# Programs without a Block, one semaphore for the last stores, one load of W2: gated hedgehog attention and MLP on one core

## The chip, the cores and the metric

The kernel runs on one core of a Trainium2 chip. The metric is the device time of one execution in microseconds (us), shown as the median of eight runs. The profile is one further view of the program: one execution recorded by the hardware profiler, with the start and the length of every instruction on the five engines and of every packet of the 16 DMA engines. TensorE is PE in the profile (its weight loads are PEld), VectorE is DVE, ScalarE is ACT, GpSimd is POOL and SyncE is SP. A "q" behind an engine's name (SPq) marks what its sequencer does by itself: issuing transfers, waiting on semaphores, draining, branching.

## What is computed

With S = 2048 rows, D = 512 columns, H = 32 heads of 16 columns, all in bf16:

```python
q, k, v = split_heads(x @ wqkv)                  # H = 32, Dh = 16
pq, pk = q @ w_phi, k @ w_phi                    # per head
phi = lambda p: concat([softmax(p), softmax(-p)])
kv = einsum("bhsf,bhsd->bhfd", phi(pk), v)       # and z: phi(pk) summed over s
o = (phi(pq) @ kv) / (phi(pq) @ z + 1e-6)
a = merge_heads(o) @ wo
b = relu(x @ w1) @ w2                            # Dff = 1376
g = sigmoid((x * gate_w).sum(-1))
return g * a + (1 - g) * b
```

A_x is the x of both branches.

## The kernel before

**How the order comes about.** Nothing schedules this kernel. The function calls `p.op`, `p.dma` and `p.wait` in the order in which each engine is to work, and `_Plan` (lines 14 to 55) keeps one list for each engine. Each entry names the events it has to wait for; `p.dma` counts 16 on the semaphore it is given, `p.op` counts 1 on its engine's. At the end `p.emit` writes one engine's list out: first the waits that this engine has not yet seen fulfilled, then the instruction. SP's list issues all transfers but two; the load of the gate's weights and the very last store are on ACT's.

**Stages.** (1) From the start to about 5 us: x arrives, TensorE runs warm-up products (line 211) and transposes the first 512 rows of x (line 217). (2) To about 18 us: the first products x @ w1 (line 499) and w_phi folded into the q and k weights (`pre`, line 281). (3) To about 83 us, the loop over 16 row tiles (line 551): `atile` (line 300) makes q and k, ACT takes exponentials, DVE sums and inverts, POOL scales, SP transposes phi(q) by DMA (line 375); `kv`, `vtile` and further `hunit`s of x @ w1 fill TensorE. (4) From about 89 us the output loop (line 584): for each row tile `nd` (numerator and denominator), `finB` (h @ w2, eleven matmuls, line 461), `finA` (o @ wo, line 470), the copy to TFA on ACT (line 475), and `comb` (line 480), in which DVE adds the two gated parts and a store goes out.

**What the change touches.** W2, the second layer of the MLP, is loaded in the middle of stage 3, at m = 3 (lines 559 to 565), by three transfers on SP's queue that share the semaphore "w2"; `finB` waits for the last of them (line 464). `comb` stores to one of three output buffers, `ob = m % 3`, each with a semaphore of its own, "out0" to "out2" (line 490), and waits for the store of tile m - 3 before it writes the buffer anew (line 487). The last tile is cut into 384 and 128 columns: the first part goes out on SP, the second on ACT (lines 598 to 602), on semaphores "out0a" and "out0b". SP ends with a wait for four events (line 603). The five lists are emitted into five bodies of one `nc.Block()` (lines 608 to 628). Entering a body is a branch on each engine; leaving the Block is a branch, a drain and a barrier of all engines, which the profile puts down to line 94, where the function's `with` closes. An opening barrier (line 642) stands before the Block and outside the function.

Of the kernel before, what the change touches and what calls it, by code (L numbers as in the profile page):

```python
# [57 lines left out]
def bass_gated_mix__linear_kernel_hedgehog__dense_activation_relu__prompt_kernel(  # L58
# [17 lines left out]
    P = 128  # L76
    NT = S // P
# [13 lines left out]
    KU = KT - 1  # L91
    NR = DFF - KU * P

    with ExitStack() as es:
        E = es.enter_context
# [8 lines left out]
        W2 = E(nc.sbuf_tensor("W2", [P, KT, D], BF16))  # L104
# [34 lines left out]
        p = _Plan(["sp", "pool", "act", "dve", "pe"])  # L139
# [6 lines left out]
        def orow(m):  # L146
            return oq[:, m, :] if m < 4 else o2[m * P:(m + 1) * P, :]
# [14 lines left out]
        for t in range(1, NDT):  # L162
            loadw1(t)
        p.dma("sp", lambda e: e.dma_start(
            out=WPS[:, :, :], in_=A_w_phi.rearrange("(g hl) r c -> (hl r) g c", g=NDT)), "wps", ev="wps")
        p.dma("sp", lambda e: e.dma_start(
            out=WV[:, :, :], in_=A_wqkv[:, 2 * D:3 * D].rearrange("(j p) n -> p j n", p=P)), "wv", ev="wv")
        for i in range(2):
            p.dma("sp", lambda e, i=i: e.dma_start_transpose(
                out=WQKT[:, 4 * i:4 * i + 4, :], in_=A_wqkv[:, i * D:(i + 1) * D]), f"wqk{i}", ev=f"wqk{i}")  # L170
        for c in range(1, NCH):
            p.dma("sp", lambda e, c=c: e.dma_start_transpose(
                out=XT[:, :, c * 512:(c + 1) * 512], in_=x2[c * 512:(c + 1) * 512, :]), f"x{c}", ev=f"x{c}")
# [9 lines left out]
            after=["wps"], ev="wd")  # L183
        for gt in range(NDT):
# [4 lines left out]
                after=["wd", "m8"], ev=f"wbd{gt}")  # L189

        p.op("dve", lambda e: e.tensor_tensor(IDN[:, :], ROWI[:, :], COLI[:, :], ALU.is_equal),
             after=["iota0"], ev="idn")
        p.op("dve", lambda e: e.tensor_single_scalar(ROW8[:, :], ROW8[:, :], 4, ALU.arith_shift_right),
             after=["iota"], ev="r8")
# [3 lines left out]
             after=["r64"], ev="m32")  # L198
# [180 lines left out]
        def vtile(m, eng="act", bank=2):  # L379
            b = m % VB  # L380
            for dt in range(NDT):
                p.op("pe", lambda e, dt=dt: e.matmul(  # L382
                    PS[:, bank, :], XT[:, dt, m * P:(m + 1) * P], WV[:, dt, :],
                    start=(dt == 0), stop=(dt == NDT - 1)),
                    after=((xready(m // 4) + ["wv"] + free[bank]) if dt == 0 else ()),
                    ev=(f"v{m}" if dt == NDT - 1 else None))
            dst, src = VS[:, b, :, 0:64], PS[:, bank, :].rearrange("p (g c) -> p g c", g=NG)
            after = [f"v{m}"] + ([f"kv{m - VB}"] if m >= VB else [])
            if eng == "dve":
                p.op("dve", lambda e: e.tensor_copy(dst, src), after=after, ev=f"cv{m}")  # L390
            else:
                p.op("act", lambda e: e.activation(dst, src, ACT.Copy), after=after, ev=f"cv{m}")  # L392
            free[bank] = [f"cv{m}"]

        def kv(m):
            b = m % NB
            vb = m % VB
            for g in range(NG):
                after = []
                if g == 0:  # L400
                    after = [f"pk{m}", f"cv{m}", f"one{vb}"]
                    if m == 0:
                        after += free[6] + free[7]
                p.op("pe", lambda e, g=g: e.matmul(  # L404
                    PS[:, 6 + g // 4, (g % 4) * GW:(g % 4) * GW + 65],
                    EB[:, b, 3, g * P:(g + 1) * P], VS[:, vb, g, 0:65],
                    start=(m == 0 and g % 4 == 0), stop=(m == NT - 1), skip_group_check=True),
                    after=after, ev=(f"kv{m}" if g == NG - 1 else None))
# [71 lines left out]
        def comb(m, cs=slice(0, 512), tag="", eng="sp"):  # L480
            ob = m % 3
            bank = fbank[(m, tag)]
            n = cs.stop - cs.start
            p.op("dve", lambda e: e.scalar_tensor_tensor(  # L484
                out=OSB[:, ob, cs], in0=PS[:, bank, 0:n], scalar=OMG[:, m:m + 1],
                in1=TFA[:, m % 2, cs], op0=ALU.mult, op1=ALU.add),
                after=[f"fb{m}{tag}", f"ta{m}"] + ([f"out{m - 3}"] if m >= 3 else []), ev=f"cb{m}{tag}")
            free[bank] = [f"cb{m}{tag}"]
            p.dma(eng, lambda e: e.dma_start(out=orow(m)[:, cs], in_=OSB[:, ob, cs]),
                  f"out{ob}{tag}", after=[f"cb{m}{tag}"], ev=f"out{m}{tag}")  # L490


        UB = (3, 4, 5, 0, 6, 7, 2, 1)
# [51 lines left out]
        def unit(c, k):  # L545
            if k < 0:
                rest(c)
            else:
                hunit(c, k)

        for m in range(NT):
            atile(m)
            if m >= LAG:
                kv(m - LAG)
            if m + 3 < NT:
                vtile(m + 3)
            for u in mid[m]:
                unit(*u)
            if m == 3:
                for i in range(2):  # L560
                    a, b = (0, 6) if i == 0 else (6, KU)
                    p.dma("sp", lambda e, a=a, b=b: e.dma_start(
                        out=W2[:, a:b, :], in_=B_w2[a * P:b * P, :].rearrange("(j p) n -> p j n", p=P)),
                        "w2", ev=f"w2{i}")
                p.dma("sp", lambda e: e.dma_start(out=W2[0:NR, KU, :], in_=B_w2[KU * P:DFF, :]), "w2", ev="w2")
            if m == 5:
                p.dma("sp", lambda e: e.dma_start(
                    out=WO[:, :, :], in_=A_wo.rearrange("(j p) n -> p j n", p=P)), "wo", ev="wo")
# [15 lines left out]
        for m in range(NT):  # L584
            if m > 1 and m + 3 < NT:
                nd(m + 3)
            if m + 1 < NT - 1:
                finB(m + 1, FB[(m + 1) % 3])
            if m == 1:
                nd(m + 3)  # L590
            if m == 0:
                nd(2)
                nd(3)
            finA(m, (6, 2, 0)[max(m - NT + 3, 0)])
            if m < NT - 1:
                comb(m)
        m = NT - 1
# [2 lines left out]
            finB(m, (4, 3)[i], cs, "ab"[i])  # L600
        for i, cs in enumerate(cuts):
            comb(m, cs, "ab"[i], ("sp", "act")[i])
        p.wait("sp", [f"out{m}" for m in range(NT - 3, NT - 1)] + [f"out{NT - 1}a", f"out{NT - 1}b"])

        sems = {}
        for name in p.count:
            sems[name] = nc.alloc_semaphore(f"s_{name}")
        block = E(nc.Block())

        @block.sync  # L610
        def _(eng):
            p.emit("sp", eng, sems)

        @block.gpsimd
        def _(eng):
            p.emit("pool", eng, sems)

        @block.scalar
        def _(eng):
            p.emit("act", eng, sems)  # L620

        @block.vector
        def _(eng):
            p.emit("dve", eng, sems)

        @block.tensor
        def _(eng):
            p.emit("pe", eng, sems)


# [26 lines left out]
```

## Time and profile before

| | us |
|---|---|
| median of 8 runs | 150.17 |
| lowest, highest of them | 149.64, 150.44 |
| the profiled execution: its time | 149.96 |
| its span, first to last instruction | 148.2 |
| busy in the span: PE | 144.0 (97%) |
| DVE | 93.2 (63%) |
| ACT | 72.1 (49%) |
| POOL | 52.1 (35%) |

The page cuts the span into 40 equal slices. A digit is the busy share of a slice in tenths, 9 meaning 90% or more; PEclk is the granted TensorE clock in tenths of full speed:

```profile
PE   7999999999999999999999999999999999999991
DVE  2427946777688878678698968655555555544242
ACT  3307627887778778887878861121111111111150
POOL 2040001788768678688869801200000000000000
PEclk9999999999999999999999999999999999999999
```

TensorE is full from the second slice to the last but one, at full clock. All the other engines have gaps. A slice is 3.7 us, so the last one, with a 1 for PE, is the time in which the output's tail leaves the chip. The page's third part names the DMA queues:

```profile
q1 hardware_dynamic: 44496, 15.92, 47.7%
q8 instruction: 8, 0.13, 0.4%
q10 hardware_dynamic: 152, 0.03, 0.1%
q14 instruction: 5, 0.04, 0.1%
```

The columns are packets, MB, and the packets' time as a share of the 16 DMA engines' span. q1 carries what SP issues, q10 what ACT issues; q8 and q14 bring the engines' own instructions.

### The profile page before, as it was taken

How to read it: one execution, taken by the hardware profiler on the slowest of the kernel's cores; microseconds unless marked ns; L12 is line 12 of the kernel's file. 1: busy time of each engine (PE TensorE's matmuls, PEld its weight loads, DVE VectorE, ACT ScalarE, POOL GpSimd, SP SyncE). 2: the span in 40 equal slices, each digit the busy share in tenths (PEclk: the TensorE clock that was granted, in tenths of full speed). 3: DMA queues.
4: the chain of work that ended last, by engine and by line, in shares of the span. 5: the costliest groups of instructions: out<-in, count | busy, mean ns of one | idle time of the engine just before them, and what ended most of it. 6: DMA issues, size and time to landing. Idle time of an engine off the chain costs nothing.

```text
span 148.2 us, 2544 instructions
## 1 busy us (share of the span) xinstructions
PE 144.0 (97%) x978; PEld 73.4 (50%) x978; DVE 93.2 (63%) x157; ACT 72.1 (49%) x123; POOL 52.1 (35%) x62
## 2 busy tenths in 40 slices
PE   7999999999999999999999999999999999999991
PEld 2544744444545545555554545554444444444451
DVE  2427946777688878678698968655555555544242
ACT  3307627887778778887878861121111111111150
POOL 2040001788768678688869801200000000000000
PEclk9999999999999999999999999999999999999999
DMA  4999993033349994335734331454142232333211
GB/s 159 293 270 213 196 221 63 0 71 71 75 82 329 183 180 74 72 70 108 75 71 95 82 71 40 89 114 116 48 98 71 71 75 71 80 91 79 71 66 47
DMA packets 44661, 16.12 MB, mean 109 GB/s; under 512 B 39304, under 2 KB 44008, under 8 KB 44648
## 3 DMA queue, kind: packets, MB, share of 16 engines
q1 hardware_dynamic: 44496, 15.92, 47.7%
q8 instruction: 8, 0.13, 0.4%
q10 hardware_dynamic: 152, 0.03, 0.1%
q14 instruction: 5, 0.04, 0.1%
HBM read 4.41 MB, written 2.10 MB: 44 GB/s over the span
## 4 chain that ended last, share of the span: by engine, by line
PE 96%; DVE 1%; issue 0%
PE PS L461 25%; PE PS L253 19%; PE PS L307 17%; PE PS L470 9%; PE PS L382 9%; PE PS L499 5%; PE PS L436 3%; PE PS L404 3%; PE PS L211 2%; PE PS L265 2%; PE PS L287 1%; PE PS L217 1%; DVE WQK L484 1%; DVE XT L227 1%; PE PS L205 0%
## 5 line engine op out<-in xcount | busy, mean ns | idle before, releaser
L461 PE MATMUL PS<-W,HT 128*128 128x512 bf16 (+4 forms) x187 | 40.6, 366 | 0.0
L326 ACT ACTIVATE EB<-PS 128x480 bf16<-128x480 f32 (+1 forms) x44 | 30.1, 756 | 15.9 <-PE PS L307 15.9
L350 POOL TENSOR_TENSOR EB<-EB,SC 128x1024 bf16<-128x1024 bf16 x15 | 28.9, 1929 | 25.1 <-DVE SC L348 25.1
L475 ACT ACTIVATE TFA<-PS,GT 128x512 bf16<-128x512 f32 x16 | 11.0, 687 | 42.7 <-PE PS L470 36.6
L253 PE MATMUL PS<-XT,W 128*128 128x512 bf16 x128 | 30.7, 379 | 0.0
L307 PE MATMUL PS<-WQK,XT 128*128 128x480 bf16 x128 | 28.5, 366 | 0.0
L484 DVE SCALAR_TENSOR_TENSOR WQK<-PS,OMG,TFA 128x512 bf16<-128x512 f32 (+2 forms) x17 | 12.2, 719 | 23.6 <-ACT TFA L475 22.4
L346 DVE TENSOR_REDUCE ZB<-EB 128x64 f32<-128x1024 bf16 x15 | 18.3, 1220 | 13.9 <-ACT EB L326 13.9
L461 PEld LDWEIGHTS PS<-W,HT 128*128 128x128 bf16 (+1 forms) x187 | 17.1, 98 | 17.4
L239 ACT ACTIVATE HT<-PS 128x512 bf16<-128x512 f32 x35 | 20.3, 614 | 7.7 <-PE PS L499 5.8
L307 PEld LDWEIGHTS PS<-WQK,XT 128*128 128x128 bf16 x128 | 12.5, 98 | 13.8
L361 DVE TENSOR_REDUCE ZB<-EB 128x64 f32<-128x1024 bf16 x16 | 18.6, 1164 | 0.0
L253 PEld LDWEIGHTS PS<-XT,W 128*128 128x128 bf16 x128 | 12.0, 98 | 13.2
L370 POOL TENSOR_TENSOR EB<-EB,SC 128x512 bf16<-128x512 bf16 x16 | 16.9, 1059 | 1.3
L382 PE MATMUL PS<-WV,XT 128*128 128x512 bf16 x64 | 16.2, 378 | 0.0
L470 PE MATMUL PS<-WO,OT 128*128 128x512 bf16 x64 | 16.1, 378 | 0.0
L446 DVE TENSOR_TENSOR WQK<-PS,RDEN 128x512 bf16<-128x512 f32 x16 | 11.1, 692 | 0.5
L470 PEld LDWEIGHTS PS<-WO,OT 128*128 128x128 bf16 x64 | 6.1, 97 | 7.2
L348 DVE RECIPROCAL SC<-ZB 128x64 f32<-128x64 f32 x16 | 8.8, 553 | 0.5
L382 PEld LDWEIGHTS PS<-WV,XT 128*128 128x128 bf16 x64 | 5.5, 97 | 4.9
L392 ACT ACTIVATE VS<-PS 128x512 bf16<-128x512 f32 x13 | 7.9, 609 | 0.0
L499 PE MATMUL PS<-XT,W 128*128 128x512 bf16 x32 | 7.6, 390 | 0.3 <-DVE XT L227 0.2
(55 smaller groups left out, 88.1 us busy)
## 6 DMA issues: line engine op xcount, KB each, us to landing
out_dram<-WQK SPq DMA_DIRECT2D x15, 128.0 KB, 1.7
W<-in_B_w_dram SPq DMA_DIRECT2D x3, 344.0 KB, 5.3
W<-in_B_w_dram SPq DMA_DIRECT2D x1, 768.0 KB, 4.8
OT<-in_A_x_dram SPq DMA_DIRECT2D x2, 256.0 KB, 2.9
WV<-in_A_wqkv_dram SPq DMA_DIRECT2D x1, 512.0 KB, 6.5
W<-in_B_w_dram SPq DMA_DIRECT2D x1, 512.0 KB, 6.1
WO<-in_A_wo_dram SPq DMA_DIRECT2D x1, 512.0 KB, 4.0
PHQ<-EB SPq DMA_TRANSPOSE x16, 2.8
```

The lines of the kernel that those rows point to most:

```text
L239: p.op("act", lambda e: e.activation(dst, src, ACT.Relu), after=[f"h{c}_{kt}"], ev=ev)
L253: p.op("pe", lambda e, t=t: e.matmul(PS[:, bank, :], W1[:, t, kt * P:(kt + 1) * P], XT[:, t, c * 512:(c + 1) * 512], start=(t == 0), stop= ...
L307: p.op("pe", lambda e, dt=dt, which=which: e.matmul(PS[:, which, 0:DE], XT[:, dt, m * P:(m + 1) * P], WQK[:, which, dt * DE:(dt + 1) * DE] ...
L326: p.op("act", lambda e: e.activation(dst, s_, ACT.Exp, scale=scale), after=[f"qk{m}"] + busy, ev=ev)
L346: p.op("dve", lambda e: e.tensor_reduce(zk, ek, AX.X, ALU.add), after=[emk, f"cst{b}"], ev=f"zk{m}")
L350: p.op("pool" if m < NT - 1 else "dve", lambda e: e.tensor_tensor(EB[:, b, 3, :].rearrange("p (g f) -> p g f", f=DH), EB[:, b, 2, :].rearr ...
L361: p.op("dve", lambda e: e.tensor_reduce(ZB[:, b, 0:64].rearrange("p (h s) -> p h s", s=2), bass.AP(tensor=EB, offset=base, ap=[[EBS, P], [ ...
L370: p.op("pool", lambda e: e.tensor_tensor(EB[:, b, 0, :].rearrange("p (h s f) -> p h s f", h=H, s=2)[:, :, 1, :], EB[:, b, 1, :].rearrange( ...
L382: p.op("pe", lambda e, dt=dt: e.matmul(PS[:, bank, :], XT[:, dt, m * P:(m + 1) * P], WV[:, dt, :], start=(dt == 0), stop=(dt == NDT - 1)), ...
L461: p.op("pe", lambda e, kt=kt, M=M: e.matmul(PS[:, bank, 0:n], HT[0:M, kt, m * P:(m + 1) * P], W2[0:M, kt, cs], start=(kt == 0), stop=(kt = ...
L470: p.op("pe", lambda e, t=t: e.matmul(PS[:, bank, :], OT[:, t, m * P:(m + 1) * P], WO[:, t, :], start=(t == 0), stop=(t == NDT - 1)), after ...
L499: p.op("pe", lambda e, u=u: e.matmul(PS[:, UB[u], :], W1[:, t, u * P:(u + 1) * P], XT[:, t, 0:512], start=(t == 0), stop=(t == NDT - 1)), ...
```

## The change

Three edits. The engines' lists are written straight into the program's main block, in the order SP, ACT, TensorE, DVE, POOL; no Block is opened, so there are no branches into bodies and no branch, drain and barrier at the end. Tiles 13, 14 and both parts of tile 15 store on one semaphore, "fin", and SP's closing wait asks for its full count (four stores of 16, so 64). The two loads of W2's full blocks (6 and 4 of them) become one of ten.

```diff
             p.dma(eng, lambda e: e.dma_start(out=orow(m)[:, cs], in_=OSB[:, ob, cs]),
-                  f"out{ob}{tag}", after=[f"cb{m}{tag}"], ev=f"out{m}{tag}")
+                  f"out{ob}" if m < NT - 3 else "fin", after=[f"cb{m}{tag}"], ev=f"out{m}{tag}")
...
             if m == 3:
-                for i in range(2):
-                    a, b = (0, 6) if i == 0 else (6, KU)
-                    p.dma("sp", lambda e, a=a, b=b: e.dma_start(
-                        out=W2[:, a:b, :], in_=B_w2[a * P:b * P, :].rearrange("(j p) n -> p j n", p=P)),
-                        "w2", ev=f"w2{i}")
+                p.dma("sp", lambda e: e.dma_start(
+                    out=W2[:, 0:KU, :], in_=B_w2[0:KU * P, :].rearrange("(j p) n -> p j n", p=P)), "w2", ev="w20")
                 p.dma("sp", lambda e: e.dma_start(out=W2[0:NR, KU, :], in_=B_w2[KU * P:DFF, :]), "w2", ev="w2")
...
-        p.wait("sp", [f"out{m}" for m in range(NT - 3, NT - 1)] + [f"out{NT - 1}a", f"out{NT - 1}b"])
+        p.wait("sp", [f"out{NT - 1}b"])
...
-        block = E(nc.Block())
-
-        @block.sync
-        def _(eng):
-            p.emit("sp", eng, sems)
...
-        @block.tensor
-        def _(eng):
-            p.emit("pe", eng, sems)
+        for name, eng in (("sp", nc.sync), ("act", nc.scalar), ("pe", nc.tensor), ("dve", nc.vector), ("pool", nc.gpsimd)):
+            p.emit(name, eng, sems)
```

The compiled lists differ from those before in nothing else: SP's has one load of W2 less, one wait in place of three entries that waited at its end, and every list is without its two branches, its closing drain and its closing semaphore entries.

More of the change, by code (lines that the diff above doesn't have):

```diff
@@ L607, in bass_gated_mix__linear_kernel_hedgehog__dense_activation_relu__prompt_kernel @@
             sems[name] = nc.alloc_semaphore(f"s_{name}")
-        block = E(nc.Block())
-        @block.sync
-        def _(eng):
-            p.emit("sp", eng, sems)
-        @block.gpsimd
-        def _(eng):
[L616 to L624, printed above, removed]
-        @block.tensor
-        def _(eng):
-            p.emit("pe", eng, sems)
+        for name, eng in (("sp", nc.sync), ("act", nc.scalar), ("pe", nc.tensor), ("dve", nc.vector), ("pool", nc.gpsimd)):
+            p.emit(name, eng, sems)
 _INS = ['A_x', 'A_wqkv', 'A_w_phi', 'A_wo', 'B_x', 'B_w1', 'B_w2', 'gate_w']
```

## The prediction

> **What bounds the kernel now.** I read the page's chain first, then the queue waits of SP, then the transfers of the last three microseconds. The chain that ended last:
>
> ```profile
> PE 96%; DVE 1%; issue 0%
> PE PS L461 25%; PE PS L253 19%; PE PS L307 17%; PE PS L470 9%; PE PS L382 9%; PE PS L499 5%; PE PS L436 3%; PE PS L404 3%; PE PS L211 2%; PE PS L265 2%; PE PS L287 1%; PE PS L217 1%; DVE WQK L484 1%; DVE XT L227 1%; PE PS L205 0%
> ```
>
> TensorE is the bound from 5 us to 145 us, and the change removes no matmul. It can therefore win only before TensorE is full or after its last matmul (issued at 144.78 us). The chain cut to the end of the run:
>
> ```profile
> 142.59 1.80 PE PS L461 x11
> 144.40 0.03 issue
> 144.42 0.62 DVE WQK L484
> 145.04 0.00 issue
> 145.04 0.35 DVE WQK L484
> ```
>
> It stops at 145.39 us, but the span is 148.16. The missing 2.76 us are two waits and the closing barrier. The waits of SP's queue after 140 us (us in total, times, longest) and the entries of L94, where a Block ends (ns, then us of first and last):
>
> ```profile
> SPq L51 <- DMA out_dram<-WQK: 2.2, 2, 1.4
> SPq L94 <- PEq L94: 0.2, 1, 0.2
> ```
>
> ```profile
> L94 POOLq EVENT_SEMAPHORE  x2: 17/17/17, 148.0 to 148.1; - x2
> ...
> L94 SPq COMPARE_BRANCH  x1: 41/41/41, 147.8 to 147.8; - x1
> L94 SPq DRAIN  x1: 7/7/7, 147.9 to 147.9; - x1
> L94 SPq EVENT_SEMAPHORE  x1: 17/17/17, 148.1 to 148.1; - x1
> ...
> L94 PEldq EVENT_SEMAPHORE  x1: 51/51/51, 148.1 to 148.1; - x1
> ```
>
> Unrounded, the records of the trace run: SP passes its wait for the store on SP at 146.771, the one for the store on ACT at 147.694 (28 ns, to 147.722), branches at 147.764, drains at 147.941; POOL gathers at 147.974 and releases at 148.052; the other engines leave from 148.094, TensorE last at 148.156.
>
> The last store is late. Issue to landing of the two kinds of store (page, part 6):
>
> ```profile
> out_dram<-WQK SPq DMA_DIRECT2D x15, 128.0 KB, 1.7
> out_dram<-WQK ACTq DMA_DIRECT2D x1, 32.0 KB, 2.3
> ```
>
> A quarter of the bytes takes 0.6 us more. The transfers between 145.4 and 147.8 us, then only those that start from 146.6 us on, say why:
>
> ```profile
> q1 hardware_dynamic: 144, 0.10, 13.3%
> q10 hardware_dynamic: 144, 0.03, 6.4%
> q14 instruction: 1, 0.01, 1.4%
> ```
>
> ```profile
> DMA packets 9, 0.00 MB, mean 1 GB/s; under 512 B 9, under 2 KB 9, under 8 KB 9
> q10 hardware_dynamic: 9, 0.00, 0.7%
> ```
>
> 144 packets of the last store are 16 DMA engines times 8 pieces and one semaphore write. All but nine run before 146.6. The nine, one engine's whole share, run from 146.993 to 147.115. The one instruction packet (8,192 B) occupies a DMA engine from 146.468 to 146.997: the store's last share starts as the fetch ends. Fifteen of the store's sixteen increments are in by 146.978, spaced about 13 ns; the last comes at 147.678. Without the fetch it would be in by some 146.99, so an instruction fetch costs the end 0.69 us.
>
> **Whose fetch it is.** Five instruction packets of 8,192 B fall in the span (TensorE has its own, 16 KB ones). Each follows a point in one engine's list of recorded instructions by 1.03 to 1.12 us, but for the first, which comes while the transfers of 44 to 49 us fill the DMA engines: DVE before its 65th and again before its 192nd, ACT before its 64th, POOL at its 68th. DVE's two are 128 apart, 64 B each. By elimination the packet at 146.468 is SP's: 1.03 us earlier SP finished issuing the 96 KB store, its 79th entry, and reached its 80th, the first final wait.
>
> **Part 1: the closing barrier, branches, Block.** Removed at the end are SP's branch and, on every engine, a drain and a semaphore wait. They lie after the last wait, on the path, with nothing beside them: 148.156 - 147.722 = **0.43 us**. At the head five branches go. Between the opening barrier's release and SP's first load lie 65 ns, between a wait and a transfer elsewhere on SP 47 (21.195 to 21.242), so a branch is worth 18 ns there; bounds 0 and 65 ns. SP's first load feeds the transposes at 3.4 us and with them TensorE's chain, so I take **0.02 us**.
>
> **Part 1b: the fetch moves.** Of the SP entries ahead of the boundary the W2 load goes once, so the 96 KB store becomes the 78th and the one wait for "fin" the 79th. The 80th is then whatever follows the kernel, and SP reaches it only when the last store has landed. A head branch that was fetched though not recorded would push the boundary one later still. No other engine gets a boundary there: ACT, at 154 entries, would have to run 38 past its end for the next one (192), POOL 107, DVE 116, TensorE some 190. So the store's last share no longer meets a fetch: **0.69 us**. The bounds are 0 (it still meets one) and 0.70; by the nearest other row, the 1.7 us of SP's stores, 145.424 + 1.70 = 147.12 and 0.56. I take 0.69, from the same store's fifteen other shares.
>
> Here a rule of the Trainium skill speaks against me: "Runtime: NRT & Kernel Launch", Instruction fetch mechanics, says that crossing a block boundary costs one bump of a DMA tail and is mostly hidden. Hidden it is for the fetching engine (SP's 80th entry ran at 146.771, before the fetch ended). It is not for the transfer behind it: 0.69 us in the trace. By the rule the sum is 0.45 us, by the trace 1.14.
>
> **Part 2: one semaphore for the last stores.** Four values are waited for now in two wait entries and a branch, afterwards one value, 64, in one entry (17 ns against 28 for the double one: 0.01 us). "DMA: Bandwidth & Descriptors", Why a DMA increments its semaphore by 16 and not by 1, warns that with two transfers in flight on one semaphore the later one's increments can let a wait pass early. That would end the run before the last byte lands. It does not bite here, because 64 is the sum of all four; by rule and trace alike the gain is 0.01. The waits at line 487 still find the earlier stores on their own semaphores, as "fin" begins at m = 13 and is waited for nowhere else.
>
> **Part 3: W2 in one load.** Issues on SP:
>
> ```profile
> L562 SPq DMA_DIRECT2D W<-in_B_w_dram x2: 532/552/573, 42.6 to 43.2; - x2
> L565 SPq DMA_DIRECT2D W<-in_B_w_dram x1: 503/503/503, 43.8 to 43.8; - x1
> ```
>
> One issue of about 0.55 us goes. SP then waits for POOL until 45.747 anyway (from 44.36), so nothing queued behind it starts earlier. The same bytes move in the same 1 KB pieces and are in by about 50.1 us (43.79 + 6.3); the first use is finB(0) at 89.28. The cover is 39 us: 0 on the path. If one larger issue cost as much as the 0.85 us of the load at L166, SP would still be done before 45.7. Its effect is on the count of SP's entries alone.
>
> **Sum.** 0.43 + 0.69 + 0.02 + 0.01 = 1.15 us. The profiled execution took 149.96 us: span 148.16 and 1.80 around it, which I leave unchanged. Afterwards: span 147.0, time 148.81. The median of the eight runs is 150.17, 0.21 above the profiled one, so against it **149.02 us**.
>
> **Rivals.**
> A, *only the barrier is won* (149.72 = 150.17 - 0.45): the store still meets a fetch, because the boundary is crossed earlier than I count, or because the collision belongs to the profiled run and not to the timed ones. For it: the fetch starts only 0.12 us before the other engines' shares are over (146.59), so a small shift decides whether they meet, and the eight runs spread by 0.8. Against it: both transfers hang on events 20 ns apart (SP done at 145.40, ACT's store issued at 145.42).
> B, *no change* (150.1): what follows the kernel waits for all engines anyway, and the 1.80 us around the span grow by what is removed. For it: 1.80 is not explained by any row. Against it: the barrier's steps stand in line after the last wait, and whatever follows came after them.
> C, *slower* (150.5): an engine that no longer stops at the barrier runs on into what follows, and its next fetch lands on a DMA engine ahead of the last store. TensorE's packets are 16 KB and took up to 1.47 us. Started at 146.3, one holds its share until 147.77; the 0.69 from there to landing, as seen (146.99 to 147.68), give 148.46 and a span of 148.5: 0.34 more, less 0.02, 150.5. It decides once the last landing slips by more than 1.15 us. Against it are the distances of 38 to 190 entries.
>
> That the edit does nothing can't be: the drains and the barrier are gone from each engine's list.
>
> **How the numbers follow.** Forecast 0.62, A 0.22, B 0.08, C 0.08. The forecast's own range is 148.75 to 149.35 (fetch term 0.56 to 0.70, and 0.2 either way for a median of eight runs that spread by 0.8, my estimate); with A it is 148.65 to 149.90, leaving out B, C and thin tails, together about 0.2. A measurement of this kernel tells about 0.2% (0.3 us) from no change. Faster: the forecast and most of A, 0.82; same: B and the rest of A, 0.10; slower: C, 0.08.
>
> **What would show it.** No L94 entry and no barrier at the end; the last entry SP's wait, within 0.05 us of the last landing; the store on ACT landing in 1.5 to 1.7 us and no instruction packet between 145.4 and 147.0; one W2 issue at 42.6 and TensorE's gaps as before. A store that still takes 2.3 us makes A right; an instruction packet of another engine there, C; a shorter span with an equal time, B.

## The result and the profile after

| | before | after |
|---|---|---|
| median | 150.12 us (32 runs) | 148.91 us (11 runs) |
| lowest, highest | 149.60, 150.63 | 148.51, 149.82 |
| profiled execution: time | 149.96 | 148.78 |
| its span | 148.16 | 146.92 |
| time minus span | 1.80 | 1.86 |

The ratio of the runs is 0.9929, with a 95% interval of 0.9912 to 0.9946: 0.7% faster. The chain that ended last, after:

```profile
PE 97%; DVE 1%; issue 0%
PE PS L461 25%; PE PS L253 19%; PE PS L307 18%; PE PS L470 9%; PE PS L382 9%; PE PS L499 5%; PE PS L436 3%; PE PS L404 3%; PE PS L211 2%; PE PS L265 2%; PE PS L287 1%; PE PS L217 1%; DVE WQK L484 1%; DVE XT L227 1%; PE PS L205 0%
```

TensorE's work is what it was. Its last weight load starts at 144.727 us before and at 144.683 after. From there to the end of the span it was 3.43 us and is 2.24. The span's gain of 1.23 us is this 1.19 and the 0.04 by which TensorE began earlier. SP's waits after 143 us (us in total, times, longest), after the change:

```profile
SPq L489 <- DVE WQK L484: 2.3, 2, 1.7
SPq L51 <- DMA out_dram<-WQK: 1.5, 1, 1.5
```

The wait for the stores was 2.2 us in two pieces; it is 1.5 in one, and the line of L94, the closing barrier, is gone. The transfers between 145.2 and 147.0 us (share of 16 engines), and the two last stores (KB, us from issue to landing):

```profile
q1 hardware_dynamic: 144, 0.10, 17.7%
q10 hardware_dynamic: 144, 0.03, 8.4%
...
out_dram<-WQK SPq DMA_DIRECT2D x1, 96.0 KB, 1.6
out_dram<-WQK ACTq DMA_DIRECT2D x1, 32.0 KB, 1.5
```

No instruction packet is among them. The store on ACT, 2.3 us before, lands after 1.5: issued at 145.381, last increment at 146.891. SP passes its wait at 146.907, leaves it at 146.924, and that is the end of the span. SP's instruction fetch is still in the records, at 148.023, 1.10 us behind the end of that wait. It is the only transfer between 147 and 149 us:

```profile
q14 instruction: 1, 0.01, 1.7%
```

### The profile page after: what moved, and what is told of

It is laid out like the page before. It is cut to its first block, busy times and chain, and to the rows that moved or that the text cites. A ratio compares the mean times of both kernels' runs of the same rounds, so it can differ in the third digit from the quotient of the medians.

```text
span 146.9 us, 2530 instructions
## 1 busy us (share of the span) xinstructions
PE 143.9 (98%) x978; PEld 73.3 (50%) x978; DVE 93.1 (63%) x157; ACT 72.1 (49%) x123; POOL 52.1 (35%) x62
## 4 chain that ended last, share of the span: by engine, by line
PE 97%; DVE 1%; issue 0%
PE PS L461 25%; PE PS L253 19%; PE PS L307 18%; PE PS L470 9%; PE PS L382 9%; PE PS L499 5%; PE PS L436 3%; PE PS L404 3%; PE PS L211 2%; PE PS L265 2%; PE PS L287 1%; PE PS L217 1%; DVE WQK L484 1%; DVE XT L227 1%; PE PS L205 0%
## 5 line engine op out<-in xcount | busy, mean ns | idle before, releaser
L253 PE MATMUL PS<-XT,W 128*128 128x512 bf16 x128 | 30.7, 379 | 0.0
L436 PEld LDWEIGHTS PS<-KVNZ,PHQ 128*128 128x128 bf16 x128 | 6.1, 97 | 3.6
```

Source lines behind the costliest of these rows:

```text
L253: p.op("pe", lambda e, t=t: e.matmul(PS[:, bank, :], W1[:, t, kt * P:(kt + 1) * P], XT[:, t, c * 512:(c + 1) * 512], start=(t == 0), stop= ...
```

## Experiments

I held two theories against each other and against a third. *Count*: the gain is the barrier and the fetch, and the fetch's place depends on nothing but how many entries SP has ahead of a fixed boundary, between its 79th and its 80th. *Barrier*: all of it comes from the Block. *Load*: fewer or larger loads on SP help as such.

One thing had to be taken out before they could be compared. From 14 us on, TensorE's list runs in lockstep in all the profiles here: its 61st weight load starts at 13.82 us before, 13.78 after, 14.12 in e1 and 13.72 in e2, and the last one keeps these distances to within 0.01 us. The differences arise between about 4 and 8.5 us, while x and W1 arrive, and they do not follow the edits: e8, the changed kernel profiled once more, has this load at 14.08. They move whole executions by some tenths of a microsecond. So the table has, beside the medians, two numbers free of that: the *tail*, from TensorE's last weight load to the end of the span in the profile, and the mean of *time minus span* over the runs. e1 to e4 ran on one chip (before: 150.09 us), e5 to e8 on another (150.18), e9 to e11 on a third (150.24).

| | Block | fetch starts, us from the last weight load | tail | time - span (runs) | both | median | ratio to before, interval |
|---|---|---|---|---|---|---|---|
| before | yes | 1.74 (in the way) | 3.43 | 1.80 (27) | 5.23 | 150.09 | |
| e1 | yes | 3.09 | 2.95 | 1.79 (16) | 4.74 | 149.56 | 0.9964 (0.9948 to 0.9980) |
| e3 | yes | 0.01 | 2.72 | 1.82 (13) | 4.54 | 149.17 | 0.9935 (0.9909 to 0.9961) |
| e6 | yes | 3.27 | 2.98 | 1.82 (21) | 4.80 | 149.78 | 0.9968 (0.9953 to 0.9983) |
| e2 | no | 1.75 (in the way) | 2.95 | 1.32 (6) | 4.27 | 149.08 | 0.9924 (0.9899 to 0.9949) |
| e4 | no | 1.76 (in the way) | 3.00 | 1.36 (6) | 4.36 | 148.90 | 0.9911 (0.9885 to 0.9936) |
| after | no | 3.34 | 2.24 | 1.83 (12) | 4.07 | 148.91 | 0.9929 (0.9912 to 0.9946) |
| e8, the same again | no | 3.33 | 2.25 | 1.83 (6) | 4.08 | 148.98 | 0.9915 (0.9888 to 0.9941) |
| e7 | no | 3.10 | 2.49 | 1.37 (6) | 3.86 | 148.65 | 0.9901 (0.9871 to 0.9931) |
| e5 | no | -0.01 | 2.24 | 1.30 (6) | 3.54 | 148.10 | 0.9873 (0.9841 to 0.9904) |

**e1: the W2 edit alone, Block kept.**

```diff
-                for i in range(2):
-                    a, b = (0, 6) if i == 0 else (6, KU)
...
+                p.dma("sp", lambda e: e.dma_start(
+                    out=W2[:, 0:KU, :], in_=B_w2[0:KU * P, :].rearrange("(j p) n -> p j n", p=P)), "w2", ev="w20")
```

> The kernel before with W2's two full-block loads made one, nothing else; Block, barrier and four final semaphores stay. Theory 'count' (a fetch of SP's instructions starts about 1.05 us after SP reaches a fixed place in its list and delays the last store by 0.7 us when it falls between 146.3 and 146.6 us): the second final wait is now at that place, it is reached only when the 96 KB store has landed at about 146.8, the fetch comes at about 147.8, the store on ACT lands in 1.5 to 1.6 us, the span is 147.4 to 147.5, the time 0.7 us below before (0.995). Rival 'barrier' (everything gained comes from the closing barrier and the Block): no change, the store on ACT still takes 2.2 to 2.3 us.

An edit 100 us ahead of the end, in a transfer that TensorE needs 40 us later, shortens the run's last two microseconds. The waits of SP after 143 us in e1:

```profile
SPq L51 <- DMA out_dram<-WQK: 1.3, 1, 1.3
SPq L94 <- PEq L94: 0.2, 1, 0.2
```

The two final wait entries themselves (ns, first and last us):

```profile
L51 SPq EVENT_SEMAPHORE  x2: 17/22/28, 147.0 to 147.5; - x2
```

One long wait is left of two, the barrier stays, and the store on ACT takes 1.54 us. The fetch came at 148.115. The rival "barrier" falls. One thing is not as expected: the tail is 2.95, only 0.48 us less than before and not 0.7. The second final wait, now behind the boundary, begins 0.444 us after the first ends (147.038 to 147.482), though its last increment had landed at 147.261. Where nothing is waited for, some 0.042 us lie between SP's entries, as between its last final wait and its branch before the change. So **crossing the boundary holds SP for 0.40 us**. Before the change the same crossing fell into a wait of 1.4 us and could not be seen.

**e2: the Block alone taken away.** Two W2 loads and four final semaphores stay.

```diff
-        block = E(nc.Block())
...
+        for name, eng in (("sp", nc.sync), ("act", nc.scalar), ("pe", nc.tensor), ("dve", nc.vector), ("pool", nc.gpsimd)):
+            p.emit(name, eng, sems)
```

> The kernel before with the lists emitted into the main block, nothing else: two W2 loads, four final semaphores. Theory 'count': the closing branch, drain and barrier go, 0.43 us. If the head branch holds no place in the list, the fetch stays where it was, the store on ACT takes 2.2 to 2.3 us, span 147.7 (0.997). If it does hold one, the place is passed one entry later, after the first final wait, the fetch misses the store and the span is 147.0 (0.9925). Rival 'barrier': the whole gain of the change, span 146.9 to 147.0, with the store's landing time no part of it.

The transfers between 144 and 147.4 us, and the stores:

```profile
q14 instruction: 1, 0.01, 0.9%
...
out_dram<-WQK SPq DMA_DIRECT2D x1, 96.0 KB, 1.7
out_dram<-WQK ACTq DMA_DIRECT2D x1, 32.0 KB, 2.2
```

The fetch is in the way as before, the store late, the span 147.6 as in the first of the two cases. So the head branches hold no place in SP's list. But the time (0.9924 and not 0.997) went below what this span allows for: time minus span fell from 1.80 to 1.32. **Without the Block the time around the span is 0.48 us shorter**, which neither theory had. With it, this one edit alone is already as fast as the whole change (0.9929).

**e3: one issue more on SP, Block kept.** WO is loaded in two halves; nothing is removed.

```diff
-                p.dma("sp", lambda e: e.dma_start(
-                    out=WO[:, :, :], in_=A_wo.rearrange("(j p) n -> p j n", p=P)), "wo", ev="wo")
+                for i in range(2):
+                    p.dma("sp", lambda e, i=i: e.dma_start(
+                        out=WO[:, 2 * i:2 * i + 2, :],
+                        in_=A_wo[2 * i * P:(2 * i + 2) * P, :].rearrange("(j p) n -> p j n", p=P)),
+                        "wo", ev=("wo0", "wo")[i])
```

> The kernel before with one issue MORE on SP: WO is loaded in two halves. It adds work and removes none. Theory 'count': the place is passed one entry earlier, when SP reaches the 96 KB store at about 143.7 and waits there for DVE; the fetch comes at about 144.7 to 145.3, before the last store's packets; the store on ACT lands in 1.5 to 1.6 us, span 147.4 to 147.5, time 0.995. Rival 'load' (the gain beyond the barrier is due to fewer or larger loads on SP): no change or slower. Rival 'barrier': no change.

The waits of SP after 143 us, then the store on ACT (min, median, max of one):

```profile
SPq L51 <- DMA out_dram<-WQK: 1.5, 2, 1.3
SPq L94 <- PEq L94: 0.2, 1, 0.2
```

```profile
DMA to landing us min/median/max: 1.5/1.5/1.5
```

Added work makes the kernel faster by 0.65%: the fetch starts at 144.709 and ends at 145.220, before the store on ACT is issued (145.396), and the crossing is hidden under SP's wait for DVE. The rival "load" falls.

**e4: the changed kernel with W2 in two loads again.**

```diff
-                p.dma("sp", lambda e: e.dma_start(
-                    out=W2[:, 0:KU, :], in_=B_w2[0:KU * P, :].rearrange("(j p) n -> p j n", p=P)), "w2", ev="w20")
+                for i in range(2):
+                    a, b = (0, 6) if i == 0 else (6, KU)
...
```

> The changed kernel with W2 in two loads again; no Block, one final semaphore. Theory 'count': the final wait is again the 80th entry of SP. If the head branch holds no place in the list, the fetch falls on the last store again, landing 2.2 to 2.3 us, span 147.6 to 147.7, 0.7 us above the changed kernel (ratio to before 0.997). If the head branch holds a place, the boundary is one later, behind the final wait, and the span stays at 146.9 (0.9925). Rival 'barrier': as the changed kernel, 146.9.

The final wait is SP's 80th entry again, and the store on ACT is late again:

```profile
SPq L51 <- DMA out_dram<-WQK: 2.3, 1, 2.3
```

```profile
DMA to landing us min/median/max: 2.3/2.3/2.3
```

The span grew by 0.7 as in the first of the two cases. Yet the time did not, and the expected ratio of 0.997 was missed: 0.9911, against 0.9929 for the changed kernel, with intervals that overlap, because time minus span fell to 1.36. Much of what the changed kernel gains inside its span by moving the fetch it loses outside. By tail and time minus span it should keep 0.29 us; the medians do not show even that, and the head's scatter is as large as this.

I then had two theories for the 1.83 of the changed kernel, and they were put against each other in e5 to e8.

**e5: no Block, and the fetch early.** The changed kernel with the edits of e4 and e3 together: W2 and WO in two loads each.

> The changed kernel (no Block, one final semaphore) with W2 AND WO each loaded in two pieces: two more issues on SP, no work removed. The instruction fetch is then due when SP reaches the 96 KB store at about 143.7 us, so it comes at about 144.7, ahead of the last store. Theory 'late fetch' (without a Block, what follows the kernel takes 1.34 us, but 1.83 when the fetch comes only after the final wait; so the changed kernel has given back 0.49 us outside its span): store on ACT 1.5 to 1.6 us, span as the changed kernel's (146.9 to 147.1), time minus span 1.3 to 1.4, time 148.3 to 148.5, ratio to before 0.989, 0.5 us below the changed kernel. Rival 'other chain' (without a Block the end of the run is set by something that does not wait for the last store, so that all these kernels end at 148.9): time 148.9, time minus span 1.8 to 1.9.

The two stores and the instruction packet between 144 and 147.4 us:

```profile
q14 instruction: 1, 0.01, 1.0%
...
out_dram<-WQK SPq DMA_DIRECT2D x1, 96.0 KB, 1.6
out_dram<-WQK ACTq DMA_DIRECT2D x1, 32.0 KB, 1.5
```

The fetch (from 144.531) is among them, but over before the last store. Tail 2.24 and time minus span 1.30: both gains at once. Its ratio is 0.9873, its median 148.10 on a chip where the changed kernel (e8) took 148.98. It beats both kernels, with two issues more on SP than the changed one; the size of its lead over that one (0.53 by the table, 0.88 by the medians of six runs each) is not well known. Rival "other chain" falls.

**e6: the changed kernel with the Block put back.**

```diff
-        for name, eng in (("sp", nc.sync), ("act", nc.scalar), ("pe", nc.tensor), ("dve", nc.vector), ("pool", nc.gpsimd)):
-            p.emit(name, eng, sems)
+        block = E(nc.Block())
...
```

> The changed kernel with the Block put back; one final semaphore and W2 in one load stay. The 80th entry of SP is now the drain behind the final wait, so the fetch comes after the last store. Store on ACT 1.5 to 1.6 us. From TensorE's last weight load to the end of the span 3.05 to 3.1 us (changed kernel 2.6), time minus span 1.8 as in all kernels with a Block, wherever their fetch fell: the time about 149.3, 0.4 above the changed kernel, ratio 0.995. If the cost of a late fetch came on top with a Block too, time minus span would be 2.2 to 2.3 and the time 149.7.

The entries of L94, where the Block ends (ns, first and last us):

```profile
L94 SPq COMPARE_BRANCH  x1: 33/33/33, 147.4 to 147.4; - x1
L94 SPq DRAIN  x1: 72/72/72, 147.8 to 147.8; - x1
```

From the branch to the drain lie 0.433 us, against 0.136 before: the boundary is crossed there, on the path, and costs 0.30. The expectation did not have this. It counted the tail from an earlier weight load than the table does; counted as in the table it stood for some 2.67 (2.24 + 0.43), and 2.98 was measured. So the kernel is not 0.4 us slower than the changed one but 0.72 by the table and 0.80 by the medians (149.78 and 148.98). The part on time minus span came true, 1.82.

**e7: the changed kernel with the four final semaphores of before.** The crossing lies between two final waits.

```diff
-                  f"out{ob}" if m < NT - 3 else "fin", after=[f"cb{m}{tag}"], ev=f"out{m}{tag}")
+                  f"out{ob}{tag}", after=[f"cb{m}{tag}"], ev=f"out{m}{tag}")
...
-        p.wait("sp", [f"out{NT - 1}b"])
+        p.wait("sp", [f"out{m}" for m in range(NT - 3, NT - 1)] + [f"out{NT - 1}a", f"out{NT - 1}b"])
```

> The changed kernel with the four final semaphores of before: no Block, W2 in one load. SP ends with two wait entries, the 79th and the 80th; the 80th is reached when the 96 KB store has landed, about 0.25 us before the last store lands. So the fetch starts at about 147.75, after the last store's packets but 0.25 us sooner than in the changed kernel (148.02). Span as the changed kernel's. Theory 'late fetch', if what follows the kernel stands still until the fetch is in: time minus span 1.55 to 1.6, time 148.65. If lateness counts only as yes or no: 1.83 and 148.9. Rival 'other chain': 148.9.

The two final wait entries (ns, first and last us):

```profile
L51 SPq EVENT_SEMAPHORE  x2: 27/28/28, 146.4 to 146.9; - x2
```

The median is the one foreseen, 148.65, but not for the reason given. Time minus span is 1.37, not 1.55 to 1.6, and the tail grew by 0.25: the second wait begins 0.445 us after the first has ended, at 146.904, with its last increment in since 146.664. So what follows does not stand still until the fetch is in (it starts at 147.538, after the span's end). SP is held at the crossing itself. In the changed kernel the crossing lies one entry later, behind the span, where no record shows it. That it costs there the 0.40 seen here is inferred; some 0.1 more of the 0.49 stays unexplained.

**e8: the changed kernel on the same chip.**

> The changed kernel itself on the same chip as the three others, for comparison: fetch after the final wait, store on ACT 1.5 us, time minus span 1.8 to 1.9, time 148.9, ratio 0.992 to 0.993.

As expected (148.98 us, time minus span 1.83).

**e9, e10, e11: which engine's end is long.** In the kernel of e5 more engines than SP wait for the last stores; no drain, branch or barrier is added.

```diff
-        p.wait("sp", [f"out{NT - 1}b"])
+        for eng in ("sp", "pool", "act", "dve", "pe"):
+            p.wait(eng, [f"out{NT - 1}b"])
```

In e10 the tuple is ("sp", "pe"), in e11 ("sp", "pool", "act", "dve").

> The two-pieces kernel of e5 (no Block, fetch early) with the final wait for the last stores put at the end of all five engines' lists and not of SP's alone; still no drain, branch or barrier. Theory 'all at once' (with a Block the time around the span is 1.80 and not 1.32 because all engines come out together, and what follows on the slowest of them is then all still to be done): time minus span 1.7 to 1.8, time 148.5 to 148.7. Rival 'instructions' (the drains, the branch or the barrier itself cost the 0.48 us outside): time minus span stays 1.3, time 148.1 to 148.2.

> As e9, but only SP and TensorE wait for the last stores. If TensorE is the engine on which the end takes longest, time minus span 1.7 to 1.8; if it is another one, 1.3.

> As e9, but SP, POOL, ACT and DVE wait and TensorE does not. If TensorE alone is the slow one, time minus span 1.3; if it is one of the others, 1.7 to 1.8.

The ends of the five lists in e9 (ns, us):

```profile
L51 SPq EVENT_SEMAPHORE  x1: 17/17/17, 147.4 to 147.4; - x1
L51 ACTq EVENT_SEMAPHORE  x1: 17/17/17, 147.4 to 147.4; - x1
L51 POOLq EVENT_SEMAPHORE  x1: 17/17/17, 147.4 to 147.4; - x1
L51 DVEq EVENT_SEMAPHORE  x1: 21/21/21, 147.4 to 147.4; - x1
L51 PEldq EVENT_SEMAPHORE  x1: 51/51/51, 147.4 to 147.4; - x1
```

In e10 only two of these entries are left:

```profile
L51 SPq EVENT_SEMAPHORE  x1: 17/17/17, 146.3 to 146.3; - x1
L51 PEldq EVENT_SEMAPHORE  x1: 51/51/51, 146.3 to 146.3; - x1
```

All come out together, without a barrier. The tails are 2.26 to 2.29, about e5's 2.24, and time minus span (four runs each) is 1.79 in e9, 1.81 in e11, and 1.55 in e10, against 1.30 in e5. The 1.55 is neither of the two values that were expected for e10. The medians are 148.93 in e9, 148.81 in e10 and 148.85 in e11 (ratios 0.9910, 0.9910, 0.9906; intervals of 0.3% either way), e9's 0.2 above what was expected.

So the rival "instructions" falls: late ends alone, without drains or a barrier, bring the 0.48 us back. If TensorE ends as late as SP, the time outside the span is 0.25 us longer; if POOL, ACT and DVE do, 0.5, and TensorE on top of them adds nothing. This fits engines that each have something to do after their lists, longer on TensorE than on SP and longest on one of POOL, ACT and DVE. It would also fit an end that takes longer the more engines come to it together (one, two, four and five of them here); no run separates the two, and which of the three engines it would be was not tried.

## Why the prediction was right

It gave 149.02 us; measured were 148.91. Step by step:

- **The closing barrier, 0.43 us in the span.** Right. Its records lay in line after the last wait and are gone; in e2, with the fetch still in the way, the tail fell by 0.48, of which 0.04 are a slightly quicker landing.
- **The fetch, 0.69 us.** Right in the span, in cause and place. The landing of the store on ACT fell from 2.254 to 1.510 us, 0.74, a little above the prediction's own upper bound of 0.70. In the time only some 0.25 of it are kept (last point). That SP's entries are what counts is shown by e1 (one less: gone), e3 (one more: gone, too, to the other side) and e4 (one back: there again).
- **The head, 0.02 us.** Nothing. SP's first load starts at 0.738 us where it started at 0.736, and e2 shows that these branches hold no place in SP's list.
- **One semaphore, 0.01 us.** Right: the last wait entry took 28 ns and takes 17.
- **W2 in one load, nothing on the path.** Right. Its issue takes 0.573 us, as that of the six blocks did, and the issue behind it 0.649 in place of 0.503. Its landing went from 6.1 at most to 7.7 us; all of W2 is in by 50.5 us, 39 us before its use.
- **The 1.80 us around the span, left unchanged.** The number held, 1.83; the step did not. Two terms that I did not have cancel. Without the Block the other engines end while SP still waits: -0.48 us (e2; e9 brings it back by late ends alone). And with the crossing of the fetch boundary pushed out of the final wait that had hidden it, the time around the span grows again: +0.49 (from 1.32 and 1.36 in e2 and e4 to 1.83), of which a hold of SP of 0.40 is seen in e1 and e7. I had argued from before's 80th entry that the fetch is hidden for SP. But that entry was a wait of 1.4 us, which would have hidden a stall of 0.4. That the two terms are of one size is luck: with either alone the forecast would have been off by half a microsecond.

By the terms it is thus -0.43 and -0.48 for the Block, -0.74 for the store, +0.49 for the crossing: -1.16, as the table's 5.23 and 4.07. The Block is thus worth 0.91 us and the moved fetch 0.25, where the prediction had 0.45 and 0.69. The trace alone could not have told the median that well; the head scatters by some tenths.

Two of the prediction's workings are off without consequence. DVE's entries before which it puts fetches, the 65th and the 192nd, lie 127 apart and not 128. And the low end of the forecast's range comes to 148.81 by its terms (149.02 - 0.01 - 0.2), not 148.75.

Rival B had the right place, the time around the span, and the wrong sign of the barrier's part. The ends of C were not reached: no other engine's fetch came near the last store. A fell with the landing of 1.5 us; that the collision belongs to the timed runs as well as to the profiled one is shown by e1 and e3, whose medians fell by 0.53 and 0.92 us with the Block in place.

## What to carry to other kernels

Look at the last two microseconds packet by packet: a store that lands late may stand behind an instruction fetch, whose place follows from the number of instructions on one engine, so that an edit far away, even one that adds work, can move it. A fetch boundary is best put under a wait that lasts anyway, ahead of the last store and not behind the last wait. And let engines that are done end: here a closing barrier cost its own records, 0.43 us, and as much again beyond the span, which early ends of the other engines saved.

## What the runs showed of the hardware

- The Trainium skill's rule ("Runtime: NRT & Kernel Launch", Instruction fetch mechanics) that a crossing is mostly hidden holds for SP here only under a wait. On the path it held SP for 0.40 us (e1, e7: 0.444 and 0.445 us between entries, against 0.042) and for 0.30 (e6: 0.433 against 0.136). SP's 8,192 B packet, 1.0 to 1.1 us later, held one DMA engine for 0.4 to 0.6 us, and in before, e2 and e4 the last store's share behind it by 0.7.
- The issue of W2's load on SP took 0.573 us for 6 blocks and for 10.
- The time outside the span depends on which, or how many, engines end last: 1.30 us where SP alone does (e5), 1.55 with TensorE (e10), 1.81 with POOL, ACT and DVE (e11), 1.79 with all (e9). It includes whatever lies ahead of the first recorded instruction, so only the differences belong to the end.
